# ScalarE, not the sync engine, issues the fetches of turned squares in later batches

## The chip, the cores and the metric

The kernel runs on one core of a Trainium2 chip. The metric is the device time of one execution in microseconds, the median over several executions. TensorE (PE in the profile) multiplies, VectorE (DVE), ScalarE (ACT) and GpSimd (POOL) work on tiles element by element, and the sync engine (SP) only issues transfers and waits. Before the change it issues every transfer of the kernel.

## The reference

Attention over a window of neighbours and over block summaries, for 4 batches of 8 heads, followed by a mixing of the tokens and a two-layer network with a residual:

```python
block, window = (32, 16)
k_sum = k.reshape(B, H, nb, block, D).max(axis=3)
v_sum = v.reshape(B, H, nb, block, D).mean(axis=3)
scores_l = scale * np.matmul(q, k.transpose(0, 1, 3, 2))          # kept where |i - j| < window
scores_s = scale * np.einsum('bhsd,bhnd->bhsn', q, k_sum) + np.log(block)
scores_all = np.concatenate([scores_l_m, scores_s], axis=-1)
a = np.exp(scores_all - max)
a = a / (np.sum(a, axis=-1, keepdims=True) + 1e-09)
attn = np.matmul(a, np.concatenate([v, v_sum], axis=2))
...
h = xt @ U @ V
u = x + h.transpose(0, 2, 1)
ch = np.maximum(u @ w_ch1, 0.0) @ w_ch2
return u + ch
```

B, H, S, D are 4, 8, 768, 64; the model width is 512, the hidden width 2048.

## The kernel before

**Stages.** The kernel works in four batches. While TensorE does the two-layer network of one batch, the attention of the next batch is woven in between: 32 steps (`later_step`), three for each head and some more at the end. The attention of batch 1 lies inside the network of batch 0 (about 95 to 200 us of the trace), that of batch 2 inside the network of batch 1 (250 to 360 us), that of batch 3 inside the network of batch 2 (405 to 520 us). In the network of batch 0 ScalarE, VectorE and GpSimd also convert the weights from 64-bit words (`L147`, `L160`, `L166`, `L169`, `L184`, `L185`) and the sync engine stores what later batches read again (tiles `up` and `down`); afterwards `whole` tiles bring the weights back and `parts` are split from them.

**Order.** Nothing is reordered by a scheduler: each engine runs its instructions in the order in which the code calls them, and each waits where it needs another's result.

**The squares.** For each head h of a later batch, TensorE makes scores (`L321`), VectorE adds the mask and takes the extreme (`L341`), and ScalarE takes exponentials (`L351`) into the tile `e`. The second product needs the exponentials turned, keys on the partitions. VectorE turns squares of 32x32 (`turn_squares`, `L371`); the squares are then moved to their places by way of DRAM: `send_squares` (`L376`) writes all of them with one transfer to the tile `there`, and `fetch_squares` (`L384`) reads them back with four transfers of 96 KB, one for each group of 32 partitions, into `at`. `square_values` (`L423`) multiplies `at` with the values `vt`. There is one buffer of `at` and one of the squares, and two of `there`.

Step h, first part, sends the squares of head h-1, fetches those of head h-2, and then makes the first half of the scores and exponentials of head h. The third part multiplies the fetched squares of head h-2, normalises, and turns the squares of head h. So a fetch has two of the three parts of a step to land in. Heads are counted from 0, batches too.

**Completion counts.** Each transfer raises one of eight counts (`DMAHW0` to `DMAHW7`) when it has landed, and a transfer that is to use a count first waits until the one before it on that count has landed. The counts are given out over all transfers of the program, whichever engine issues them.

**The network's ScalarE work.** `L803` and `L1135` make the gate's upper part `gh`, VectorE makes the lower part `gl` from it (`L804`, `L1136`). In batch 0 the second product (`L813`) of one half follows after the first product (`L791`) of the next half; in later batches (`L1151`) the gate is made one block of hidden units ahead.

Of the kernel before, what the change touches and what calls it, by code (L numbers as in the profile page):

```python
# [84 lines left out]
def body(ctx: ExitStack, tc, q0, q1, k, v, vn, uv, w1, w2, mask, ident, rep, out):  # L85
    nc = tc.nc
# [292 lines left out]
    def fetch_squares(st, h):  # L379

        there = st.at[h].rearrange("(i k) j c -> j k i c", k=32)
        at = st.at[h] = att.tile([P, 4, NU, 32], F32, name="at", bufs=1)
        for j in range(4):
            nc.sync.dma_start(  # L384
                out=at[32 * j : 32 * j + 32].rearrange("k i u q -> k i (u q)"), in_=there[j]
            )

# [85 lines left out]
    def later_step(st, i):  # L473
# [5 lines left out]
        if a == 0:  # L479
            if 1 <= h <= H:  # L480
                send_squares(st, h - 1)
            if 2 <= h <= H + 1:
                fetch_squares(st, h - 2)
            if h < H:
                scores(st, h, 0)
                exponentials(st, h, 0)
            if 3 <= h <= H:
                load_v(st, h - 1)
        elif a == 1:
            if h < H:  # L490
                scores(st, h, 1)
                exponentials(st, h, 1)
            if h + 1 < H:
                key_maxima(st, h + 1)
            if 1 <= h <= H:
                for t in range(2):
                    value_summaries(st, h - 1, t, nc.scalar.copy)
        else:
            if h + 2 < H:
                load_qk(st, h + 2)  # L500
            if h == 2:
                st.x = mo.tile([P, NU, DM], F32, name="x")
            if 2 <= h <= H + 1:
                square_values(st, h - 2)
                normalise(st, h - 2)
            if h < H:
                turn_squares(st, h)
# [800 lines left out]
```

## Time and profile before

| | |
|---|---|
| Time, median of 3 runs | 677.57 us (676.94 to 678.1) |
| The profiled execution's time | 678.02 us |
| its span | 676.2 us |
| TensorE busy | 641.9 us, 95% |
| VectorE, GpSimd, ScalarE busy | 386.6, 372.0, 343.1 us |
| Transfers of `at`, all issued by the sync engine | 96 of 96 KB |

Times in the trace count from the span's start. In rows of the timeline and of the chain the first number is the start and the second the duration; a bracket at the end gives how long the engine stood idle ahead of it and who ended that. "SPq" is an issue of the sync engine. In rows of stretches each engine's busy time is followed by its number of instructions in brackets, then the granted share of TensorE's clock, the busy share of the 16 DMA engines, and GB/s. "Landing" is the time from the start of an issue to the transfer's completion, as minimum, median and maximum. A wait is put down to the semaphore that came last, so an engine that happens to have finished just then can be named in place of a transfer.

### The profile page before, as it was taken

How to read it: one execution, taken by the hardware profiler on the slowest of the kernel's cores; microseconds unless marked ns; L12 is line 12 of the kernel's file. 1: busy time of each engine (PE TensorE's matmuls, PEld its weight loads, DVE VectorE, ACT ScalarE, POOL GpSimd, SP SyncE). 2: the span in 40 equal slices, each digit the busy share in tenths (PEclk: the TensorE clock that was granted, in tenths of full speed). 3: DMA queues.
4: the chain of work that ended last, by engine and by line, in shares of the span. 5: the costliest groups of instructions: out<-in, count | busy, mean ns of one | idle time of the engine just before them, and what ended most of it. 6: DMA issues, size and time to landing. Idle time of an engine off the chain costs nothing.

```text
span 676.2 us, 13190 instructions
## 1 busy us (share of the span) xinstructions
PE 641.9 (95%) x4800; PEld 568.2 (84%) x4800; DVE 386.6 (57%) x1041; ACT 343.1 (51%) x751; POOL 372.0 (55%) x428
## 2 busy tenths in 40 slices
PE   5889997989999899999999999999999999999997
PEld 4768796879888799998877899998877899998886
DVE  3778798777898666555655634566654432232222
ACT  3855356355433556665453467665543365553322
POOL 5846967635697757651245486661334375563420
PEclk9999999899999999999999999999999999999999
DMA  9999679898992169785438059777432144431002
GB/s 250 249 345 279 218 231 297 252 272 305 279 330 100 52 185 309 209 250 151 143 104 248 23 174 311 229 222 220 127 97 79 55 148 165 139 126 62 32 0 94
DMA packets 82752, 124.47 MB, mean 184 GB/s; under 512 B 7680, under 2 KB 57728, under 8 KB 82688
## 3 DMA queue, kind: packets, MB, share of 16 engines
q1 hardware_dynamic: 82688, 123.63, 60.3%
q8 instruction: 38, 0.62, 0.4%
q14 instruction: 26, 0.21, 0.1%
HBM read 96.34 MB, written 27.26 MB: 183 GB/s over the span
## 4 chain that ended last, share of the span: by engine, by line
PE 75%; DMA 11%; DVE 6%; ACT 3%; SPq 2%; POOL 2%; issue 1%; ACTq 0%; POOLq 0%; DVEq 0%
PE acc L1151 27%; PE ps_h L1066 24%; PE acc L813 7%; PE ps_h L791 6%; PE ps_s L321 4%; PE ps_x L423 3%; DMA place<-in_q 2%; DMA qz<-in_q 2%; PE ps_o L610 2%; DMA place<-in_w 1%; DMA at<-there 1%; DMA place<-in_v 1%; DVE gl L1136 1%; DMA kt<-in_k 1%; DMA place<-in_k 1%
## 5 line engine op out<-in xcount | busy, mean ns | idle before, releaser
L185 POOL TENSOR_TENSOR parts<-whole,parts 128x512 fp32r<-128x512 f32 (+1 forms) x144 | 181.6, 1270 | 165.6 <-ACT parts L184 137.1
L1151 PE MATMUL acc<-parts,gh 128*128 128x512 f32 x576 | 193.4, 399 | 0.0
L1066 PE MATMUL ps_h<-op,parts 128*128 128x384 f32 x1008 | 188.4, 339 | 1.2 <-POOL parts L185 0.6
L1066 PEld LDWEIGHTS ps_h<-op,parts 128*128 128x128 f32 x1008 | 173.6, 188 | 3.1 <-POOL parts L185 0.9
L1151 PEld LDWEIGHTS acc<-parts,gh 128*128 128x128 f32 x576 | 108.1, 188 | 22.9 <-issue 0.8
L1151 PE MATMUL acc<-parts,gl 128*128 128x512 f32 x288 | 113.1, 393 | 1.9 <-DVE gl L1136 1.9
L1136 DVE SCALAR_TENSOR_TENSOR gl<-place,gh 128x768 fp32r<-128x768 f32 x48 | 58.9, 1228 | 83.1 <-ACT gh L1135 83.0
L184 ACT CAST parts<-whole 128x512 fp32r<-128x512 f32 (+1 forms) x144 | 83.5, 583 | 5.8 <-DMA whole<-up 4.3
L351 ACT ACTIVATE e<-e,neg 128x120 f32<-128x120 f32 x144 | 46.5, 386 | 59.7 <-DVE neg L341 53.6
L791 PE MATMUL ps_h<-place 128*128 128x384 f32 x384 | 74.3, 341 | 1.2 <-DVE place L592 0.5
L813 PE MATMUL acc<-place,gh 128*128 128x512 f32 x192 | 68.3, 411 | 2.1 <-POOL place L185 2.1
L791 PEld LDWEIGHTS ps_h<-place 128*128 128x128 f32 x384 | 66.6, 188 | 4.2 <-DVE place L592 1.3
L1135 ACT ACTIVATE gh<-place 128x768 fp32r<-128x768 f32 x48 | 40.6, 846 | 55.1 <-PE acc L1151 54.9
L1151 PEld LDWEIGHTS acc<-parts,gl 128*128 128x128 f32 x288 | 54.2, 188 | 13.1 <-DVE gl L1136 3.9
L160 POOL TENSOR_SCALAR val<-place 128x512 f32<-128x512 f32 (+1 forms) x30 | 48.7, 1638 | 29.6 <-ACT place L147 17.7
L185 POOL TENSOR_TENSOR place<-val,place 128x512 fp32r<-128x512 f32 x29 | 38.6, 1351 | 19.5 <-ACT place L184 19.5
L185 POOL TENSOR_TENSOR op<-tmp,op 128x384 fp32r<-128x384 f32 x24 | 24.5, 1030 | 42.7 <-ACT op L184 38.5
L341 DVE CUSTOM_DVE_ANT_0 e<-ps_s,mask_sb 128x120 f32<-128x120 f32 x144 | 32.9, 278 | 25.3 <-PE ps_s L321 24.5
L813 PEld LDWEIGHTS acc<-place,gh 128*128 128x128 f32 x192 | 36.6, 192 | 11.1 <-POOL place L185 3.4
L803 ACT ACTIVATE gh<-ps_h 128x384 fp32r<-128x384 f32 x32 | 15.6, 488 | 54.3 <-PE ps_h L791 54.1
L321 PEld LDWEIGHTS ps_s<-kt,qz 128*128 128x128 f32 x288 | 39.0, 191 | 4.4 <-DVE kt L303 1.6
L321 PE MATMUL ps_s<-kt,qz 128*128 128x120 f32 x288 | 39.7, 274 | 2.0 <-DVE kt L303 1.2
(110 smaller groups left out, 848.4 us busy)
## 6 DMA issues: line engine op xcount, KB each, us to landing
place<-in_w SPq DMA_DIRECT2D x32, 512.0 KB, 6.0
whole<-up SPq DMA_DIRECT2D x24, 512.0 KB, 4.0
whole<-down SPq DMA_DIRECT2D x24, 512.0 KB, 3.7
there<-squares SPq DMA_DIRECT2D x24, 384.0 KB, 4.2
at<-there SPq DMA_DIRECT2D x96, 96.0 KB, 3.9
whole<-up SPq DMA_DIRECT2D x24, 384.0 KB, 3.5
vt<-in_v SPq DMA_DIRECT2D x48, 146.2 KB, 4.0
kt<-in_k SPq DMA_DIRECT2D x24, 288.0 KB, 5.6
```

The costliest lines, as they stand in the source:

```text
L160: nc.gpsimd.tensor_scalar(f32(bits), f32(hi), 0.0, None, ALU.mult)
L184: nc.scalar.copy(hi, val)
L185: engine.tensor_tensor(lo, val, f32(hi), ALU.subtract)
L321: nc.tensor.matmul(ps[:, i * KC : (i + 1) * KC], qt[:, 64 + j * P : 64 + j * P + P], kt[:, k0 : k0 + KC], start=True, stop=True,)
L341: nc.vector.tensor_tensor_reduce(out=e[:, i, :], in0=ps[:, i * KC : (i + 1) * KC], in1=mask_sb[:, m, :], scale=-SCALE, scalar=BIG, op0=ALU ...
L351: nc.scalar.activation(e[:, i, :], e[:, i, :], AF.Exp, bias=st.neg[h][:, u : u + 1], scale=-1.0,)
L791: nc.tensor.matmul(ps[:, :NH], w_split[0, f][:, c % 2, part_w, c // 2], ut[:, c, :], start=(n == 0), stop=(n == 3 * NC - 1),)
L813: nc.tensor.matmul(acc[t], gt[:, sl], w_split[1, f][:, part_w], start=(first and j == 0), stop=(last and j == 2),)
L1066: nc.tensor.matmul(ps, a[:, sa, i], b[:, sb, i], start=(first and n == 0), stop=(n == 5), skip_group_check=not first,)
L1135: nc.scalar.activation(gh, h, AF.Relu)
L1136: nc.vector.scalar_tensor_tensor(gl, h, 0.0, f32(gh), ALU.max, ALU.subtract)
L1151: nc.tensor.matmul(acc[t], gt[:, sl], w[:, part_w], start=(f == 0 and j == 0), stop=(f == NF - 1 and j == 2),)
```

## The change

One word changes: the four transfers of a fetch are issued by ScalarE. The send stays with the sync engine.

```diff
@@ fetch_squares
         at = st.at[h] = att.tile([P, 4, NU, 32], F32, name="at", bufs=1)
         for j in range(4):
-            nc.sync.dma_start(
+            nc.scalar.dma_start(
                 out=at[32 * j : 32 * j + 32].rearrange("k i u q -> k i (u q)"), in_=there[j]
             )
```

In the sync engine's order before, around the fetch of head 1 of the first later batch (`there_1338` is the squares of that head, `up2_111` a store of converted weights):

```order
L213 DMA qz0_83<-in_q1 64x4x128 [waits DMAHW7_49]
L725 DMA down2_119<-val_1220 128x512 [waits DMAHW0_49,DVE_49]
L728 DMA up2_111<-place_1263 128x1024 [waits DMAHW1_49]
L376 DMA there_1483<-squares_1457 128x768 [waits DMAHW2_49,DVE_49]
L384 DMA at_1485<-there_1338 32x4x192 [waits DMAHW3_49,PE_49]
L384 DMA at_1485<-there_1338 32x4x192 [waits DMAHW4_49]
L384 DMA at_1485<-there_1338 32x4x192 [waits DMAHW5_49]
L384 DMA at_1485<-there_1338 32x4x192 [waits DMAHW6_49]
L227 DMA vt_1503<-in_v 96x390 [waits DMAHW7_49,Activation_49]
```

The fetch stands behind the send of the next head's squares, which waits for VectorE. The same place in ScalarE's order afterwards, and in the sync engine's:

```order
L184 CAST place_1403<-val_1220 128x512
L184 CAST place_1406<-val_1219 128x2x256
L803 ACTIVATE gh_1479<-ps_h_1466 128x384 [waits PE_49,Activation_49]
L384 DMA at_1485<-there_1338 32x4x192 [waits DMAHW6_49,DMAHW5_49,DMAHW7_49,DMAHW3_49,DMAHW2_49]
L384 DMA at_1485<-there_1338 32x4x192 [waits DMAHW4_49]
L384 DMA at_1485<-there_1338 32x4x192 [waits DMAHW6_49]
L384 DMA at_1485<-there_1338 32x4x192 [waits DMAHW1_49]
```

```order
L725 DMA down2_119<-val_1220 128x512 [waits DMAHW0_49,DVE_49]
L728 DMA up2_111<-place_1263 128x1024 [waits DMAHW1_49]
L376 DMA there_1483<-squares_1457 128x768 [waits DMAHW3_49,DVE_49]
L227 DMA vt_1503<-in_v 96x390 [waits DMAHW5_49,PE_49,Activation_49]
L228 DMA vt_1503<-in_v 96x390 [waits DMAHW7_49]
```

The four transfers have moved between the gate `gh` and the exponentials of head 3 (`L351`). The fourth waits on `DMAHW1`, which `up2_111` uses just before it.

In batch 2, around the fetch of head 7 (`at_4460`), ScalarE's four transfers and then the sync engine's order afterwards:

```order
L384 DMA at_4460<-there_4311 32x4x192 [waits DMAHW4_49,DMAHW3_49,DMAHW7_49,DMAHW2_49,DMAHW1_49]
L384 DMA at_4460<-there_4311 32x4x192
L384 DMA at_4460<-there_4311 32x4x192 [waits DMAHW4_49]
L384 DMA at_4460<-there_4311 32x4x192 [waits DMAHW5_49]
```

```order
L748 DMA whole_4324<-down7_124 128x1024 [waits DMAHW0_49,Pool_49]
L748 DMA whole_4430<-up0_109 128x1024 [waits DMAHW4_49,Pool_49]
L253 DMA stage_4487<-in_vn 128x512 [waits DMAHW5_49]
L253 DMA stage_4489<-in_vn 128x512 [waits DMAHW6_49]
L206 DMA kt_4491<-in_k 128x3x192 [waits DMAHW7_49]
```

Before, the four stood between `whole_4430` and `stage_4487` on the sync engine. Now the third waits for `whole_4430` (`DMAHW4`) and the fourth for `stage_4487` (`DMAHW5`), both issued by the sync engine.

## Prediction

> **What bounds the kernel now.** I read the page first, then the stretches in which the change acts, then who waits for the tile `at`.
>
> ```profile
> span 676.2 us, 13190 instructions
> ...
> PE 641.9 (95%) x4800; PEld 568.2 (84%) x4800; DVE 386.6 (57%) x1041; ACT 343.1 (51%) x751; POOL 372.0 (55%) x428
> ...
> DMA  9999679898992169785438059777432144431002
> ...
> PE 75%; DMA 11%; DVE 6%; ACT 3%; SPq 2%; POOL 2%; issue 1%; ACTq 0%; POOLq 0%; DVEq 0%
> ```
>
> TensorE is busy for 95% of the span and the chain that ended last is three quarters TensorE, so only what opens or closes a hole in TensorE's row moves the end. ScalarE works half of the time.
>
> ```profile
> core 0: us, PE busy (x) PEld busy (x) DVE busy (x) ACT busy (x) POOL busy (x), PEclk, DMA share, GB/s
> 95.00:200.00 105.00, 97.22 (x874) 84.94 (x873) 84.28 (x228) 53.70 (x120) 67.97 (x65) 0.97 0.94 289
> 250.00:360.00 110.00, 108.51 (x952) 96.08 (x951) 63.84 (x193) 62.58 (x137) 54.57 (x62) 1.00 0.67 199
> 405.00:520.00 115.00, 114.07 (x1000) 100.81 (x999) 62.98 (x194) 65.72 (x144) 55.52 (x63) 1.00 0.64 190
> ```
>
> These three stretches hold the fetches of batches 1, 2 and 3, eight each. TensorE's holes are 7.8, 1.5 and 0.9 us. Only in batch 1 is there something to win, and there the DMA engines are 94% busy. The view of the tile `at` says how much of it belongs to the fetch:
>
> ```profile
> L384 SPq DMA_DIRECT2D at<-there x96: 303/432/1736, 100.4 to 509.9; - x96
> ...
>   DMA at<-there: 3.8, 2
>   DVE val L166: 2.7, 2
> ...
> DMA to landing us min/median/max: 2.2/3.9/7.2
> ```
>
> TensorE waited for the fetch twice, 3.8 us in all. One of the waits put down to `val` L166 belongs to it too (below). Issuing a transfer takes the sync engine 432 ns in the median, landing takes 2.2 to 7.2 us more.
>
> **The change part by part.** Removed from the sync engine: 96 issues, 24 groups of four. Added to ScalarE: the same 96, each with its wait. I price an issue there at the same 0.43 us, the nearest row, since ScalarE issues nothing now; the bounds are 0.30 and 1.74 us from the same row. A group is 4 x 0.43 = 1.7 us of ScalarE's sequencer, 24 x 1.7 = 41 us against some 330 us in which ScalarE is idle. The issues stand just ahead of a head's exponentials, and there ScalarE usually waits anyway, as at head 0 of batch 2:
>
> ```profile
> 264.49 0.68 ACT L351 ACTIVATE e<-e,neg 128x120 f32<-128x120 f32 x2 [1.45 <-POOL parts L185]
> ```
>
> So the issue time itself costs nothing at most places. If that cover is gone, the exponentials slip by 1 to 2 us, and what follows is the transposition on VectorE, one head ahead of need.
>
> What costs is the wait in each transfer. A transfer raises one of eight completion counts and first waits for the landing of the one before it on that count. Those eight are now shared by two engines' orders, so ScalarE stands still for transfers of the sync engine. I took each of the 24 groups, looked up in the order whose landing it needs, and set the landing in the trace against TensorE's use. Fifteen groups come out with a microsecond or more to spare, or with no later issue than now. Head 3 of batches 2 and 3 must wait for the send of the current squares and keeps a few tenths (0 each, up to +0.8 if landing takes a microsecond more). The other seven follow.
>
> *Batch 1, head 1 (the long wait).* The chain of waits, cut to 95:130:
>
> ```profile
> 105.04 7.59 DMA qz<-in_q
> ...
> 112.65 4.88 DMA at<-there
> ...
> 117.66 1.53 PE ps_x L423 x48
> 119.19 3.95 PE acc L813 x9
> ...
> 125.89 2.08 PE acc L813 x9
> ```
>
> Now the fourth transfer goes out at 112.65, when a `qz` load has landed, and lands at 117.53; TensorE starts at 117.66 after 3.65 us of nothing. In the changed order the fourth transfer waits for the store `up2_111`:
>
> ```profile
> L728 SPq DMA_DIRECT2D up<-place x1: 442/442/442, 107.3 to 107.3; - x1
> ...
> DMA to landing us min/median/max: 7.5/7.5/7.5
> ```
>
> 107.35 + 7.5 = 114.9. Allowing 0.5 us for the first transfers now going beside that store, the issue is at 115.4. A lighter queue lands a fetch in 2.9 us (head 3, below), so it lands at 118.3: 0.8 us later than now. Lower bound 114.9 + 2.2 = 117.1 (0.4 earlier); upper 115.9 + 3.9 = 119.8 (2.3 later). I take +0.8, since it goes out into a queue of its own.
>
> Behind those transfers stand, on ScalarE:
>
> ```profile
> 108.60 0.49 ACT L803 ACTIVATE gh<-ps_h 128x384 fp32r<-128x384 f32 x1 [0.96 <-PE ps_h L791]
> 110.00 0.97 ACT L351 ACTIVATE e<-e,neg 128x120 f32<-128x120 f32 x3 [0.91 <-DVE neg L341]
> 110.88 1.22 ACT L147 ACTIVATE place<-place 128x512 f32<-128x512 f32 x2
> 112.28 0.97 ACT L351 ACTIVATE e<-e,neg 128x120 f32<-128x120 f32 x3 [0.18 <-DVE neg L341]
> 113.27 1.04 ACT L307 COPY vt<-vsum 24x390 f32<-24x390 f32 x2
> 114.22 0.47 ACT L803 ACTIVATE gh<-ps_h 128x384 fp32r<-128x384 f32 x1
> ```
>
> Their work, 0.97 + 1.22 + 0.97 + 1.04 + 0.47 = 4.7 us, would start at 115.8 instead of 110.00, and `gh` would be done at 120.5 instead of 114.7. VectorE waits there for `gh`. The accumulation that reads it is the one that the chain shows at 125.89, so 5 us are left: no cost. VectorE's transposition slips by about 1.5 us and with it the next send, which the fourth transfer of head 2 needs; that one keeps a few tenths (0, bounds 0 and +0.6).
>
> *Batch 1, head 3.*
>
> ```profile
> 135.44 2.50 SPq L384 DMA_DIRECT2D at<-there  x4
> ...
> DMA to landing us min/median/max: 2.3/2.9/3.4
> ...
> 132.82 1.14 ACT L184 CAST place<-val 128x512 fp32r<-128x512 f32 x2 [1.41 <-DVE val L169]
> ...
> 140.49 0.73 PE L423 MATMUL ps_x<-vt,at 120*32 120x65 f32 x37 [1.17 <-DVE val L166]
> ```
>
> The last transfer goes out at 137.5 and lands 2.8 us later, at 140.3; TensorE starts at 140.49. L166 makes weights that this product does not read, and it had just ended, so I read the 1.17 us as the fetch's. The sync engine reaches the group only at 135.44, behind the send of the current squares. ScalarE's last wait ahead of the group ends at 132.8 and the counts that it needs are landed by then or a microsecond later, so the fetch lands near 138: -1.1 us (bounds -1.2 and 0, if L166 was the releaser after all).
>
> *Batch 1, head 4.* The third and fourth transfers wait for a `kt` load and a store; ScalarE stands for 1 to 3 us, the fetch lands about when it does now: 0 (bounds -0.2 and +1.3, the copy of `mix_t` coming late).
>
> *Batch 1, head 7.* The fourth transfer waits for the load of `vt`:
>
> ```profile
> 197.62 0.60 PE L423 MATMUL ps_x<-vt,at 120*32 120x65 f32 x27
> ...
> L227 SPq DMA_DIRECT2D vt<-in_v x1: 338/338/338, 191.5 to 191.5; - x1
> ...
> DMA to landing us min/median/max: 4.4/4.5/4.5
> ```
>
> 191.5 + 4.4 = 195.9, then 2.3 to 2.9 us to land: 198.2 to 198.8, 0.6 to 1.2 us after TensorE wants it. That load goes out up to 1.1 us earlier when the sync engine has no fetch to issue, which takes most of it back: +0.3 (bounds 0 and +2.5).
>
> *Batch 2, head 7.*
>
> ```profile
> 352.50 0.34 SPq L748 DMA_DIRECT2D whole<-up  x1
> 353.02 1.75 SPq L384 DMA_DIRECT2D at<-there  x4
> 354.82 0.91 SPq L253 DMA_DIRECT2D stage<-in_vn  x2
> ...
> 358.59 0.89 PE L423 MATMUL ps_x<-vt,at 120*32 120x65 f32 x48
> ...
> DMA to landing us min/median/max: 3.6/3.6/3.6
> ...
> DMA to landing us min/median/max: 3.8/3.8/3.8
> ```
>
> The two last lines are the landing of `whole` and of the first `stage`. Now nothing holds the fetch. Changed, its third transfer waits for that `whole` (352.50 + 3.6 = 356.1) and its fourth for `stage`, which goes out at 352.9 once the fetch is gone but stands behind `whole`: at 356.7, by the rate at which these transfers land now. So it is issued at 356.8 and lands 2.2 to 2.9 us later, at 359.0 to 359.7; with the 0.13 us from landing to start, 0.5 to 1.3 us after 358.59. I take +0.9 (bounds +0.5 and, with 3.8 us, +2.2). Batch 3's head 7 has no such wait: its counts have landed long before. 0 (bounds 0 and +0.5).
>
> What the sync engine gains, 24 x 2 us, is worth nothing by itself: in the three stretches no other hole of TensorE ends with a load.
>
> Whether a fetch from a second issuer lands in 2.9 us or in the 3.9 us of all fetches decides three of these terms. The Trainium skill, "DMA: Bandwidth & Descriptors", section "Issuing engines are not separate DMA queues", speaks for the slower value: all issuers' transfers run on the same 16 engines and interleave, and a second issuer saves only sequencer time, which is small. By it the sum would be that of the slower rival below, +4.9 us in place of +0.9; the trace, with one issuer, cannot show which.
>
> Sum, heads 1, 2, 3, 4 and 7 of batch 1, then heads 7: 0.8 + 0 - 1.1 + 0 + 0.3 + 0.9 + 0 = +0.9 us. All lower bounds together give -1.3 us, all upper ones some +11. The profiled execution took 678.02 us, the median of the runs is 677.57, 0.07% apart, so I set it on the median: 678.5 us. A change of under 0.2% (1.36 us) can't be told from none in this kernel; the forecast is one of those.
>
> **The rivals.**
>
> *Faster: head 1 of batch 1 stops costing.* TensorE's clock in the window after that wait:
>
> ```profile
> 116.00:122.70 6.70, 5.04 (x56) 4.14 (x57) 3.75 (x8) 1.14 (x2) 6.54 (x7) 0.50 0.92 273
> ```
>
> The granted clock was 0.50: the nine accumulations took 3.95 us there against 2.08 at 125.89, and 48 products 1.53 against the 0.89 seen at 358.59. That is 1.87 + 0.64 = 2.5 us on top of the wait. If the fetch lands at 116 or before (its store and loads landing earlier because the sync engine is two microseconds ahead), the wait shrinks by 1.5 us or more and the slow clock may not come: -1.5 - 2.5 - 1.1 + 1.2 = -3.9, 673.7 us. For it: the sync engine does lose 2 us of issuing per head. Against it: at 94% busy the DMA engines, not the issues, set those landings. It decides when the wait falls below some value between the 1.17 us that left the clock alone and the 3.65 us that did not. The Trainium skill, "TensorE: Matmul & The Clock Gate", section "Why this matters for your kernels", puts that value at about 3 us; the trace agrees as far as its two waits go.
>
> *Slower: the shared completion counts.* The three late groups land by the median of all fetches, 3.9 us, rather than 2.9: head 1 at 119.3 (+1.8), head 7 of batch 1 at 199.8 (+2.2), head 7 of batch 2 at 356.8 + 3.7 (+2.0). With head 3's -1.1 that is +4.9, 682.5 us. It decides at about 3.1 us, where the sum passes 1.36. For it: the fetch's own median. Against it: that median was made in one ordered queue, where a fetch stands behind all the rest.
>
> *Nothing happens:* all fetches stay hidden, or gains and losses cancel: 677.6 us, within my own range.
>
> **How the numbers follow.** Forecast with its cancelling terms (676.3 to 678.9) 0.45; the faster rival 0.20; the slower 0.35, since there are more late groups than early ones. Hence faster 0.20, same 0.45, slower 0.35. The range reaches into both rivals until a tenth is left on each side: 674.8 to 682.0. The likeliest case's own is 676.3 to 678.9.
>
> **What would show it.** Right: TensorE's wait at head 1 of batch 1 stays between 3 and 5 us with its stretch of half clock; the 1.17 us at head 3 is gone; a new hole of about a microsecond at head 7 of batch 2; ScalarE standing some 5 us at head 1 with the exponentials behind it, and no accumulation waiting for `gl` because of it. Wrong: no slow-clock stretch at all; ScalarE's issues much dearer than 0.43 us; holes at batch 2 and 3 heads that I gave a microsecond to spare; or exponentials so late that the sends, and the fetches behind them, slip head by head.

## The result, and the profile after

The kernel became slower: 700.72 us (697.75 to 703.22) against 677.84 us of the kernel before, measured with it, a ratio of 1.0335 (95% interval 1.0285 to 1.0384). The forecast was 678.5 us, at most 682.0. The profiled execution of the changed kernel took 697.75 us, 19.7 us more than that of the kernel before; the median is 3 us higher still, and the runs spread more.

The page of the changed kernel: the span, the engines' busy time, the load of the DMA engines in slices, and the transfer queues (q1 is the sync engine's, q10 ScalarE's new one).

```profile
span 696.0 us, 13207 instructions
...
PE 646.4 (93%) x4800; PEld 570.6 (82%) x4800; DVE 385.4 (55%) x1041; ACT 341.1 (49%) x751; POOL 370.5 (53%) x428
...
DMA  9999599787982169784437239878332045441002
...
q1 hardware_dynamic: 68864, 114.19, 53.4%
q10 hardware_dynamic: 13824, 9.44, 5.1%
...
PE 65%; DMA 14%; DVE 7%; POOL 5%; ACT 3%; issue 3%; SPq 2%; ACTq 0%; POOLq 0%; DVEq 0%
```

TensorE does the same 4800 products. It is busy 4.5 us longer and the span is 19.8 us longer, so some 15 us are new holes and the rest slower products. The chain that ended last went from 75% TensorE to 65%, and DMA from 11% to 14%.

The view of the tile `at`, in the changed kernel:

```profile
L384 ACTq DMA_DIRECT2D at<-there x96: 309/442/1837, 95.0 to 530.5; - x96
...
  DVE gl L804: 11.3, 3
  DMA at<-there: 7.8, 3
...
  ACT e L351: 23.8, 7
...
DMA to landing us min/median/max: 1.9/4.8/7.9
```

An issue costs ScalarE 0.44 us, what it cost the sync engine. A transfer lands 4.8 us after its issue in the median instead of 3.9. And ScalarE's exponentials (`e`, `L351`) now stand idle 23.8 us behind the fetch's transfers, at seven places. The 11.3 us put down to `gl` are three waits of products and weight loads at heads 1 and 7 of batch 1; there the fetch landed 0.1 us ahead of TensorE's start, and `gl` happened to end next to it.

### The profile page after: what moved, and what is told of

It is laid out like the page before. It is cut to its first block, busy times and chain, and to the rows that moved or that the text cites. A ratio compares the mean times of both kernels' runs of the same rounds, so it can differ in the third digit from the quotient of the medians.

```text
span 696.0 us, 13207 instructions
## 1 busy us (share of the span) xinstructions
PE 646.4 (93%) x4800; PEld 570.6 (82%) x4800; DVE 385.4 (55%) x1041; ACT 341.1 (49%) x751; POOL 370.5 (53%) x428
## 4 chain that ended last, share of the span: by engine, by line
PE 65%; DMA 14%; DVE 7%; POOL 5%; ACT 3%; issue 3%; SPq 2%; ACTq 0%; POOLq 0%; DVEq 0%
PE acc L1151 26%; PE ps_h L1066 22%; PE acc L813 5%; PE ps_s L321 4%; DMA at<-there 4%; PE ps_x L423 3%; PE ps_h L791 2%; DMA qz<-in_q 2%; DMA place<-in_w 2%; PE ps_o L610 2%; DMA whole<-up 1%; DMA place<-in_v 1%; POOL val L160 1%; DMA place<-in_q 1%; POOL place L185 1%
## 5 line engine op out<-in xcount | busy, mean ns | idle before, releaser
L351 ACT ACTIVATE e<-e,neg 128x120 f32<-128x120 f32 x144 | 46.4, 386 | 72.9 <-DVE neg L341 35.5
```

Of the source, the lines that this page charges most:

```text
L351: nc.scalar.activation(e[:, i, :], e[:, i, :], AF.Exp, bias=st.neg[h][:, u : u + 1], scale=-1.0,)
```

## Where the time went

Both traces hold the same 4800 products in the same order, so each product's start can be taken in both and subtracted. The difference is -1.6 us ahead of the first fetched squares (it arose before 60 us of the trace, where no fetch is issued) and +19.7 us at the end: 21.3 us to explain. It moves at few places only:

| place (time in the trace after) | grows by, us | what ended TensorE's wait |
|---|---|---|
| batch 1, head 0 (104.04) | +0.35 | the fetch |
| batch 1, heads 1 and 3 (116.49, 138.07) | +0.1, -1.2 | the fetch; the hole of 1.17 us is gone |
| mixing (143 to 148) | +0.5 | late `gl` and `t` |
| batch 1, head 4 (152.17) | +2.0, and +1.5 slow clock | the fetch |
| products with converted weights (164.5 and 165.9; 183.2 and 187.0) | +1.4; +1.3 | `place`, late from ScalarE and GpSimd; at 183.2 (0.3 us) `gl` |
| batch 1, head 7 (205.09) | +3.15 | the fetch |
| first product of a block (267.58) | +1.2 | a `whole` load |
| batch 2, head 3 (317.49) and mixing (325.94) | +0.6, +1.1 | the fetch; late exponentials |
| batch 2, head 7 (373.32) | +4.4, and +1.9 slow clock | the fetch |
| batch 3, head 1 (456.43) | +0.4 | the fetch |
| batch 3, head 3 (482.50) and mixing (490.95) | +1.5, +1.1 | the fetch; late exponentials |

Late fetches 12.4 us, the slow clock behind two of them 3.4, work that ScalarE did late 5.4, a load 1.2, a gain of 1.1 at heads 1 and 3: 21.3 us. The load of 1.2 us has no fetch near it, and that hole, 0.54 us in the kernel before and 1.74 here, is 2.0 and 1.4 us in experiments 3 and 9, which lost nothing; its cause is left open.

At head 4 the profile puts the wait down to `val`:

```profile
152.17 1.51 PE L423 MATMUL ps_x<-vt,at 120*32 120x65 f32 x48 [2.13 <-DVE val L166]
```

This product does not read `val`. The fetch's last transfer landed at 151.97, 0.20 us ahead of the product, as at head 3 in the kernel before (140.29 and 140.49), so the wait is counted as the fetch's. The 48 products take 1.51 us in place of 0.89: the slow clock.

The timeline of the changed kernel at the largest place, head 7 of batch 2 (start, duration, engine; the bracket is the idle time ahead and who ended it):

```profile
362.84 0.34 SPq L748 DMA_DIRECT2D whole<-up  x1
...
363.24 0.91 SPq L253 DMA_DIRECT2D stage<-in_vn  x2
...
364.08 0.31 ACTq L384 DMA_DIRECT2D at<-there  x1
...
364.42 0.45 ACTq L384 DMA_DIRECT2D at<-there  x1
...
366.35 2.28 ACTq L384 DMA_DIRECT2D at<-there  x2
...
368.67 0.62 ACT L184 CAST parts<-whole 128x512 fp32r<-128x512 f32 x1 [3.06 <-DMA stage<-in_vn]
...
373.32 0.98 PE L423 MATMUL ps_x<-vt,at 120*32 120x65 f32 x28 [4.33 <-DMA at<-there]
```

The third transfer waits for `whole` until 366.3, the fourth for the first `stage` until 368.3: the two waits that the order had shown. Each issue starts 0.02 us after that landing. The view of `at`, cut to that fourth transfer, and the same for the fourth transfer of head 7 of batch 1 (issued at 199.5, when a `vt` load has landed):

```profile
L384 ACTq DMA_DIRECT2D at<-there x1: 309/309/309, 368.3 to 368.3; - x1
...
DMA to landing us min/median/max: 4.9/4.9/4.9
```

```profile
L384 ACTq DMA_DIRECT2D at<-there x1: 310/310/310, 199.5 to 199.5; - x1
...
DMA to landing us min/median/max: 5.4/5.4/5.4
```

At head 4 of batch 1 it is 6.4 us, at head 1 5.4. The waits are about where they were put; the landing behind them takes twice what was counted.

What late ScalarE work does is seen at 145 to 166 us:

```profile
145.98 0.96 ACT L351 ACTIVATE e<-e,neg 128x120 f32<-128x120 f32 x3 [4.16 <-DMA at<-there]
...
163.00 0.97 ACT L351 ACTIVATE e<-e,neg 128x120 f32<-128x120 f32 x3 [3.18 <-DMA at<-there]
...
163.88 1.12 ACT L184 CAST place<-val 128x512 fp32r<-128x512 f32 x2
...
164.57 2.53 POOL L185 TENSOR_TENSOR place<-val,place 128x512 fp32r<-128x512 f32 x2 [8.81 <-ACT place L184]
...
165.90 0.73 PE L813 MATMUL acc<-place,gh 128*128 128x512 f32 x2 [0.63 <-POOL place L185]
```

ScalarE stands 4.2 and 3.2 us at the fetch's transfers, the conversion of weights behind it is late, GpSimd waits for it, and TensorE for GpSimd.

## The experiments

Theory A: a fetch's transfers wait for transfers of the sync engine by the shared counts, so the fetch lands late. Theory B: what costs is ScalarE, which stands at those waits and does its other work late. Theory C: a second issuer's queue lands slower, whatever it waits for. Each ratio is to runs of the kernel before on the same chip.

**1. The fetch behind the exponentials.**

```diff
@@ later_step, a == 0
-            if 2 <= h <= H + 1:
-                fetch_squares(st, h - 2)
             if h < H:
                 scores(st, h, 0)
                 exponentials(st, h, 0)
+            if 2 <= h <= H + 1:
+                fetch_squares(st, h - 2)
```

> ScalarE still issues all fetches, but behind the step's scores and exponentials instead of ahead of them, so the exponentials no longer stand behind the transfers' waits. Theory A (late landing: the shared completion counts send out a fetch's last transfer late, and TensorE waits for it): the order puts more fetches behind a load that the sync engine issues later (heads 1, 2, 4 of batch 1, head 3 of batches 2 and 3 now wait for a vt load), so the holes at the product with the fetched squares stay or grow: 700 to 708 us. Theory B (late ScalarE: what costs is that exponentials and gates stand behind the fetch): most of the 23 us comes back: 680 to 687 us.

Measured 720.73 us, 1.0615 (1.0577 to 1.0654), above both expectations. TensorE waits 2.4 to 5.1 us at eight heads, among them two whose fourth transfer now waits for a `vt` load (5.0 us at head 3 of batch 1, 4.1 at head 3 of batch 3; at head 3 of batch 2, 3.3 us, the load had landed 1.2 us before the fourth went out). The edit did two things, freeing the exponentials and sending the fetch out later; together they cost 20 us more than the change. What the first is worth alone can't be read here.

**2. The fetch a part earlier.** At the end of the third part, just behind the product that frees `at`.

```diff
@@ later_step, a == 0
-            if 2 <= h <= H + 1:
-                fetch_squares(st, h - 2)
@@ later_step, a == 2
                 normalise(st, h - 2)
+            if 1 <= h <= H:
+                fetch_squares(st, h - 1)
             if h < H:
                 turn_squares(st, h)
```

> ScalarE still issues all fetches, but at the end of the step's third part, directly behind the product that frees the one buffer of at, instead of at the start of the next step: about 4 us more lead. ScalarE now also waits there for TensorE. Theory A (late landing): the holes at heads 4, 7 of batch 1 and head 7 of batch 2 (2.1, 3.1 and 4.3 us, with 3.4 us of slow clock) close, 682 to 688 us, and 678 if the hole at head 1 closes too. Theory B (late ScalarE): ScalarE stands as long as before and for TensorE besides: 698 to 706 us.

Measured 694.54 us, 1.0223 (1.0196 to 1.0249): between the two. The fetches land in time (the one wait at `ps_x` that is new takes 0.8 us), but ScalarE now stands up to 6 us for its transfers, and TensorE waits for late `gl` and `gh` instead, 4.8 us in one place. One loss was turned into the other, so neither theory holds alone.

**3. The sync engine, fetch ahead of send.** The kernel before with the two calls swapped.

```diff
@@ later_step, a == 0 (of the kernel before)
-            if 1 <= h <= H:
-                send_squares(st, h - 1)
             if 2 <= h <= H + 1:
                 fetch_squares(st, h - 2)
+            if 1 <= h <= H:
+                send_squares(st, h - 1)
```

> The sync engine issues everything, as before the change, but the fetch of a head goes ahead of the send of the next head's squares instead of behind it. This is the part of the change that takes the fetch out from behind the send, without a second issuer. Theory A (the loss is all the second issuer's shared counts): the wait of 1.17 us at head 3 of batch 1 goes, head 1 gains up to 2 us: 674 to 677.5 us. Rival (any earlier place of the fetch delays the send by 2 us, and with it the next fetch): 678 to 681 us.

Measured 673.79 us, 0.9934 (0.9907 to 0.9962): faster, by 0.7%. The products with the fetched squares of heads 1, 2 and 3 of batch 1:

```profile
113.29 0.89 PE L423 MATMUL ps_x<-vt,at 120*32 120x65 f32 x48 [1.35 <-DMA at<-there]
...
123.98 0.89 PE L423 MATMUL ps_x<-vt,at 120*32 120x65 f32 x48
...
133.68 0.54 PE L423 MATMUL ps_x<-vt,at 120*32 120x65 f32 x22 [0.96 <-DMA at<-there]
```

The long wait at head 1 fell from 3.65 to 1.35 us, and its 48 products take 0.89 us, not 1.53: full clock. The gain of getting out from behind the send was there to be had, without a second issuer.

**4. Four heads back to the sync engine.**

```diff
@@ fetch_squares
+        issuer = nc.sync if (st.b, h) in ((1, 1), (1, 4), (1, 7), (2, 7)) else nc.scalar
         for j in range(4):
-            nc.scalar.dma_start(
+            issuer.dma_start(
```

> ScalarE issues all fetches but four: heads 1, 4 and 7 of batch 1 and head 7 of batch 2 are issued by the sync engine again, at their old place, where each transfer waits for the one eight before it. Theory A (late landing at the groups whose counts belong to a later or slow transfer): the holes and slow clock of heads 4 (3.5 us) and 7 (3.15 us) of batch 1 and head 7 of batch 2 (6.3 us) go: 700.7 - 13 = 687.8 us, between 684 and 690. Theory B (each group costs ScalarE time, 23 us over 24 groups): 700.7 - 4 x 0.96 = 696.9 us, between 695 and 699.

Measured 687.53 us, 1.0126 (1.0079 to 1.0172): Theory A's number. At those four heads no wait of TensorE over 0.03 us is left. New ones of 2.7 and 4.5 us came at heads 0 and 2 of batch 1, and with them other counts: which head is hit hangs on how the counts fall.

**5 and 6. One transfer per fetch, by ScalarE and by the sync engine.** The squares lie in DRAM in the order in which they are read.

```diff
@@ send_squares
-        nc.sync.dma_start(out=there, in_=st.at[h].rearrange("p j u q -> p j (u q)"))
+        squares = st.at[h].rearrange("p j u q -> p j (u q)")
+        for i in range(4):
+            nc.sync.dma_start(
+                out=there[:, i].rearrange("(j k) c -> k j c", k=32), in_=squares[32 * i : 32 * i + 32]
+            )
@@ fetch_squares (nc.sync in the control)
-        there = st.at[h].rearrange("(i k) j c -> j k i c", k=32)
+        there = st.at[h]
...
-        for j in range(4):
-            nc.scalar.dma_start(
-                out=at[32 * j : 32 * j + 32].rearrange("k i u q -> k i (u q)"), in_=there[j]
-            )
+        nc.scalar.dma_start(out=at.rearrange("k i u q -> k i (u q)"), in_=there)
```

> The squares are laid out in DRAM so that a fetch is one transfer of 384 KB (3 KB a partition) instead of four; the send becomes four transfers of 96 KB on the sync engine. ScalarE still issues the fetch, at the same place in its order. By the order, a fetch now raises one count, and the transfer before it on that count was given out 11 to 20 transfers earlier (3 earlier at head 7 of batch 2, 8 at head 7 of batch 3), instead of 1 to 8 earlier or even behind it. Theory A (the waits for the shared counts are the loss): TensorE's holes at heads 4 and 7 of batch 1 and head 7 of batch 2 go, and with them the late exponentials: 674 to 682 us. Theory C (a second issuer's queue lands slower, whatever it waits for: 4.8 us in the median against 3.9): the fetches stay late, 690 to 700 us.

> The control of the run before: the same layout, four sends and one fetch, all issued by the sync engine, the fetch behind the sends as in the kernel before. Theory A: no second issuer, so near the kernel before; head 1 of batch 1 keeps most of its wait: 676 to 681 us. Theory C: the same. If this one is far from the kernel before, the layout itself matters, and the run before is to be read against this one.

Measured 685.69 us, 1.0092 (1.0061 to 1.0122), and for the control 679.28 us, 0.9985 (0.9963 to 1.0007). No effect of the layout by itself is seen. With ScalarE, one transfer, and so one count, instead of four took away about two thirds of the loss; the rest stands between the theories' ranges. The edit also took three of four issues off ScalarE, so it does not single out the counts; that issues by themselves cost little is shown by experiment 9, where fifteen groups of four lose nothing. The timeline with ScalarE at head 2 of batch 1, where TensorE still waits:

```profile
119.63 0.38 SPq L227 DMA_DIRECT2D vt<-in_v  x1
...
124.39 0.55 SPq L657 DMA_DIRECT2D place<-in_w  x1
...
124.77 0.49 ACT L804 ACTIVATE gh<-ps_h 128x384 fp32r<-128x384 f32 x1 [3.75 <-PE ps_h L792]
...
124.95 0.36 ACTq L387 DMA_DIRECT2D at<-there  x1
...
132.74 0.56 PE L424 MATMUL ps_x<-vt,at 120*32 120x65 f32 x12 [2.57 <-DMA at<-there]
```

Between the two quoted lines of SPq the sync engine issues six more loads and stores. ScalarE reaches the fetch only behind the gate, which waited 3.75 us for TensorE, so the fetch goes out behind eight transfers, six of them still on their way, and lands 7.7 us later; the sync engine's own, at 122.7 in the control, took 4.6.

**7. One transfer, sync engine, fetch first.** The control with the swap of experiment 3.

> Everything on the sync engine, one transfer per fetch, and the fetch ahead of the sends. The version with the fetch of four transfers ahead of the send measured 0.9934 of the kernel before. If fewer counts help on one issuer too, the remaining waits at heads 1 and 3 of batch 1 (1.35 and 0.96 us there) go: 670 to 673 us. If the sends, now four issues of which the last lands later, take that back: 674 to 678 us.

Measured 672.49 us, 0.9886 (0.9857 to 0.9916): the fastest version, 1.1% ahead of the kernel before. One wait for the fetch is left, 1.65 us at head 1 of batch 1; against experiment 3 the difference is within what the two intervals leave open.

**8. One transfer, ScalarE, a part earlier.** Experiment 5 with the move of experiment 2.

> ScalarE issues the fetch as one transfer, at the end of the step's third part, directly behind the product that frees the one buffer of at, instead of at the start of the next step. With one transfer at the old place (685.7 us, 1.0092 of the kernel before) the fetch of head 2 of batch 1 went out only when ScalarE had done the gate gh ahead of it, behind seven loads that the sync engine had already issued, and landed 7.7 us later. Theory D (what is left of the loss is the place in ScalarE's order, behind work that waits for TensorE): the holes of 2.2, 2.6 and 1.5 us at heads 1 and 2 of batch 1 and head 7 of batch 2 shrink, 672 to 679 us. Theory C (ScalarE's queue lands slower, by 0.5 to 2 us): 682 to 688 us, since the transfers then still land late at heads 1 and 2, and ScalarE waits for TensorE besides.

Measured 678.67 us, 1.0000 (0.9974 to 1.0025): Theory D's. ScalarE can issue the fetches at no loss, if one count is waited for and the place is early. It is still 6 us behind the sync engine in experiment 7: TensorE waits 2.6 us for the fetch at head 1 of batch 1, and 1.1 and 1.2 us for `gl`.

**9. Fifteen groups on ScalarE.** Four transfers each, the other nine back on the sync engine.

```diff
@@ fetch_squares
+        back = {1: (0, 1, 2, 4, 7), 2: (3, 7), 3: (1, 3)}
+        issuer = nc.sync if h in back[st.b] else nc.scalar
```

> Four transfers per fetch; nine of the 24 groups, those at which TensorE had a hole in the changed kernel or in the version with four heads back (heads 0, 1, 2, 4, 7 of batch 1, 3 and 7 of batch 2, 1 and 3 of batch 3), are issued by the sync engine, the other 15 by ScalarE. Theory A (the loss sits in the groups whose counts belong to slow or later transfers; the others are free): 676 to 681 us. Theory B (each group costs ScalarE time, 23 us over 24 groups): 677.8 + 15 x 0.96 = 692 us.

Measured 680.89 us, 1.0015 (0.9985 to 1.0045): no difference from the kernel before, 11 us under Theory B. Its one long wait is the kernel before's own, 3.82 us at head 1 of batch 1:

```profile
118.26 1.05 PE L425 MATMUL ps_x<-vt,at 120*32 120x65 f32 x29 [3.82 <-DMA at<-there]
```

The loss sat in nine groups out of 24.

**10 and 11. ScalarE only stands.** The fetches are the sync engine's, as in experiment 3; ScalarE copies a few numbers of the fetched tile to DRAM, so it stands there until the fetch has landed, in the second version until the first of the four transfers has.

```diff
@@ fetch_squares (of experiment 3), behind the four transfers
+        stand = dram.tile([P, 4], F32, name="stand")
+        nc.scalar.dma_start(out=stand, in_=at[:, 0, 0, :4])          # 10
+        nc.scalar.dma_start(out=stand, in_=at[:32, 0, 0, :4])        # 11, with 32 rows in stand
```

> The price of ScalarE standing, without a late fetch: the sync engine issues the fetches, ahead of the sends (the version that measured 0.9934 of the kernel before), and ScalarE, at the place where the changed kernel has its fetch, issues one transfer of 2 KB that copies four numbers a partition of the fetched tile to DRAM, so that it stands there until the fetch has landed, then goes on to its exponentials. By that version's trace it stands 3 to 5 us at each of the 24 heads, as long as in the changed kernel in batch 1 and longer in batches 2 and 3. Theory A (late fetches are the loss of the changed kernel, ScalarE's standing is worth the 6 us that the late weights and mixing show): 676 to 684 us, between 2 and 10 us over 673.8. Theory B (ScalarE's standing is the loss): 690 us or more. If standing costs nothing: 672 to 676 us.

Measured 701.53 us, 1.0339 (1.0277 to 1.0401): Theory B's number, 27.7 us over experiment 3. TensorE has hardly a wait for a fetch; it waits for the lower gates and the mixing. The timeline at 117 to 123 us:

```profile
117.37 0.34 ACTq L388 DMA_DIRECT2D stand<-at  x1
...
117.83 0.97 ACT L351 ACTIVATE e<-e,neg 128x120 f32<-128x120 f32 x3 [5.40 <-POOL e L336]
...
121.75 0.47 ACT L805 ACTIVATE gh<-ps_h 128x384 fp32r<-128x384 f32 x1
...
122.26 0.56 DVE L806 SCALAR_TENSOR_TENSOR gl<-ps_h,gh 128x384 fp32r<-128x384 f32 x1 [2.45 <-ACT gh L805]
...
122.87 0.79 PE L793 MATMUL ps_h<-place 128*128 128x384 f32 x3 [2.17 <-DVE gl L806]
```

The gate `gh` comes behind the exponentials, `gl` behind `gh`, and TensorE's next first product `ps_h` waits for `gl`: `gl` reads the `ps_h` of before, and the banks are given out in turn.

So standing by itself can cost as much as the change did, if it is long enough. It is not quite alone: the added transfers take counts too, and an issue of the sync engine started just as one of them landed twice here and nine times in experiment 11. But from 95 us on no hole of TensorE that is new against experiment 3 ends with a load in either trace. How long: the idle time ahead of ScalarE's instruction behind each transfer, less the idle time ahead of the same instruction in the kernel before, summed where it is positive, is 56 us here and 24 us in the changed kernel. Hence the shorter one:

> As the run before (701.5 us), but ScalarE's small transfer copies numbers of the first 32 partitions alone, so ScalarE stands only until the first of the fetch's four transfers has landed: some 2 us less at each head. In the run before ScalarE stood idle at those places 56 us longer than in the kernel before, in the changed kernel 24 us longer; here it should be 15 to 30 us. Theory A (in the changed kernel standing is worth the 5 to 7 us of holes that end with late work of ScalarE, and the rest of the loss is late fetches): 676 to 682 us, 3 to 8 over 673.8. Theory B (each us of extra standing costs half a us, as in the run before: 27.7 for 56): 673.8 + 0.49 x 24 = 685.6 us, between 683 and 689. If the cover in front of the exponentials takes it all: 672 to 676 us.

Measured 688.76 us, 1.0165 (1.0125 to 1.0206), 15.0 us over experiment 3, with 35 us of extra standing: in Theory B's range, above Theory A's. That is 0.43 us lost for each us. But the 35 us were read in the fastest of its five executions (684.25 us), and from 95 us on that trace lost 10.8 us against experiment 3's, 0.31 for each; in experiment 10 the same two ways give 0.49 and 0.44. In experiment 9 the extra standing is 4 us.

What follows: the shared counts cost twice. They hold back the fetch, and they hold up ScalarE. In the changed kernel the holes that a fetch ended, with their slow clock, are 15.8 us, those that ScalarE's late work ended 5.4 us. By experiments 10 and 11, 24 us of standing would be worth 7 to 12 us with the fetches in time. The difference is not settled: part of a hole that a late fetch ends may cover late work of ScalarE.

Why the fetch lands late, once issued, can be counted in the traces. A transfer is on its way from the start of its issue until it lands. Of the fetches' 96 transfers in the kernel before, 36 went out while at most one transfer that was not a fetch's was on its way (median landing 3.3 us) and 27 while four or more were (5.1 us and up). In the changed kernel these are 14 and 45, and the median with four or five others is 5.6 us. The sync engine no longer holds its loads behind the fetch, while the counts hold the fetch's last transfers back until those loads are out. At equal crowding the two kernels differ by half a microsecond at most, so little is left for Theory C. That is a count, not an experiment: holding the sync engine back to see the landing shorten was not tried.

## Why the prediction was wrong

**Right.** The mechanism and its places: the shared counts, with `whole` and `stage` at head 7 of batch 2, `vt` at head 7 of batch 1 and a store at head 4. The gain of 1.1 us at head 3 of batch 1 came (1.2). An issue costs 0.44 us. Most groups are hidden: experiment 9 puts fifteen at nothing (not quite the same fifteen; head 1 of batch 3 and head 0 of batch 1, which the forecast had among them, cost 0.4 each). No loss at head 7 of batch 3.

**Near by luck.** The wait at head 1 of batch 1 is 3.77 us, between the 3 and 5 us that were forecast; its term was +0.8 and it grew by 0.1. But two errors cancelled. The fourth transfer went out at 111.05, some 3 us earlier than counted with the traces' offset of 1.3 us taken off: the store that it waits for went out 1.1 us earlier and landed in 6.1 us, not 7.5. Then it landed in 5.4 us instead of 2.9.

**The step that failed first: the landing.** "A lighter queue lands a fetch in 2.9 us" was read off one fetch that had waited behind a send, while the queue emptied. The last transfers measured 6.4 us (head 4), 5.4 (head 7 of batch 1) and 4.9 (head 7 of batch 2). The terms were 0, +0.3 and +0.9 us; their holes grew by 2.0, 3.15 and 4.4, all above their upper bounds of 1.3, 2.5 and 2.2. (For head 4 the forecast wrote no landing down; the last issue was 0.6 us later than before and its landing 1.3 us longer.) Heads 3 of batches 2 and 3, priced at 0 and at most +0.8, grew by 0.6 and 1.5: their last transfers wait for the send, as said, but land in 4.3 and 5.1 us. At head 7 of batch 2 the issue was also 1.2 us later than counted: at 368.3, less the 10.3 us by which this place had already slipped, 358.0 for 356.8. The slower rival had the right mechanism and ran out of size: it used 3.9 us, the median of the kernel before, and gave +4.9 in place of 21.3. The Trainium skill, "DMA: Bandwidth & Descriptors", section "Issuing engines are not separate DMA queues", stood on its side: the transfers interleave on the same engines, and a second issuer saves sequencer time alone. The trace agrees, 0.43 us an issue saved on the sync engine and 3.9 us of landing turned into 4.8.

**Second: standing.** "So the issue time itself costs nothing" holds, but the wait in front of it does not pass unseen. The forecast put ScalarE's stops at no cost, because the one accumulation looked at had 5 us to spare. It left out the converted weights behind `place` (+2.7 us), the mixing (+2.7), and that a first product `ps_h` can wait for `gl`. Experiments 10 and 11 price it at 0.3 to 0.5 us for each extra us.

**Third: the clock.** No price was set for a new slow stretch, since no new hole over 1.3 us was forecast. Head 4 of batch 1 and head 7 of batch 2 brought two, 3.4 us together.

The chances went wrong with the first step. The lower bounds came from the emptiest moments of the trace, the upper ones stopped at the median, while the trace's own maximum, 7.2 us, was in sight. One reading was loose: landing takes 2.2 to 7.2 us from the start of the issue, not on top of it; the sums use it rightly.

## What to carry to other kernels

Where transfers of two engines share completion counts, moving some to a second engine makes each wait for the other's: look up whose landing every moved transfer needs, and take for its own landing what the queue shows when it is full. A compute engine that issues transfers stands at each such wait with all its later work, and idle time in front of one instruction is cover for that instruction's wait alone. What the change was after, a fetch no longer behind the send, came from two lines in another order on the same engine (0.9934), and with fewer transfers per fetch 0.9886.

## What the runs showed of the hardware

TensorE's clock did not fall at one length of hole. Windows of the changed kernel behind the holes at head 4 (2.13 us, ended at 152.17), head 7 of batch 1 (3.14 us, ended at 205.09) and head 7 of batch 2 (4.33 us, ended at 373.32); the last three numbers are the granted clock, the share of the DMA engines and GB/s:

```profile
152.00:154.00 2.00, 1.83 (x49) 1.69 (x50) 0.78 (x3) 0.08 (x1) 2.00 (x2) 0.56 0.30 101
...
205.00:209.00 4.00, 3.90 (x82) 2.99 (x82) 2.81 (x9) 0.60 (x2) 3.75 (x5) 1.00 0.96 342
...
373.00:377.00 4.00, 3.68 (x53) 3.13 (x54) 0.91 (x3) 0.00 (x0) 0.00 (x0) 0.50 0.99 290
```

The hole of 2.13 us was followed by half clock, the one of 3.14 us was not. In the traces of the kernel before, the changed one and all eleven experiments, from 95 us on, each of the 14 holes of 3.3 us and more was followed by half clock, eleven of the fourteen between 2.1 and 3.2 us were, and of those between 1.1 and 2.1 us only one, of 1.58 us. What decides between 2.1 and 3.2 us was not looked into. The Trainium skill, "TensorE: Matmul & The Clock Gate", section "Why this matters for your kernels", gives about 3 us of idle; here it began at 2.1, once at 1.6.
